# Mem rows turned with six products, ones written as four-byte words, and a new order for units 0 to 2

## The chip, the cores and the metric

The kernel runs on one core of a Trainium2 chip. The metric is the device time of one execution in microseconds (us). The kernel before takes 224.45 us, the median of three runs (224.44 to 224.99). A core has five engines that each work through a queue of their own in order: PE (matrix products; its weight loads run ahead of them), DVE (vector operations), ACT (activations, copies), POOL (vector operations; here it also issues nearly all loads) and SP (here it issues stores and a few copies). They wait for each other by semaphores.

## The reference

Two layers on 4 sequences of 768 tokens, 8 heads of 64 values. First a chunked attention: queries of a chunk of 32 tokens see 8 memory rows, 16 tokens to the left of the chunk, the chunk, and 8 tokens to the right.

```python
k_full = np.concatenate([mem_k, k_ctx], axis=2)
v_full = np.concatenate([mem_v, v_ctx], axis=2)
scores = scale * np.matmul(q_c, k_full.transpose(0, 1, 3, 2))
a = np.exp(scores - np.max(scores, axis=-1, keepdims=True))
a = a / (np.sum(a, axis=-1, keepdims=True) + 1e-09)
out[:, :, c_start:c_end] = np.matmul(a, v_full)
```

Then, with the heads side by side (512 values for each token), a normalised two-layer network with a residual:

```python
xn = (x - mu) / np.sqrt(var + 1e-06) * g_ln
out = x + np.maximum(xn @ w_ch1, 0.0) @ w_ch2      # 512 -> 2048 -> 512
```

## The kernel before

Tokens are worked in 24 blocks `t` of 128 (six for each sequence `b`), and the network in 12 units `u` of 256 tokens, so unit `u` has blocks 2u and 2u+1. One block goes through these steps, each a small function:

- `qk_products(t)` (PE, 32 small matmuls, L322): scores from the turned queries `QD` and the turned keys `KT`; `row_max` and `less_max` (DVE, L331 and L334); `weights` (ACT, exp, L344).
- `pt_products(t)`, `pt_copy`: the weights turned on PE and copied out of PSUM (L353, L361).
- `val_products(t)` (PE, L373): weights by `V`. `V` has a column of ones beside each head's values, so that the same product gives the sum of the weights. `tokens(t)` (DVE, L382 to L389) divides by it and takes the mean.
- `shift(t)` (POOL L396 or ACT L400) subtracts the mean, `x_products` turns the block on PE (L429), `x_copy` (DVE, L445) takes it out of PSUM into `xT`. `square` (ACT) and `root_of` (POOL) make the scale that is applied at the very end.

A unit then has eight `up_products(u, s)` (PE, L464, 8 matmuls of 256 columns each), each followed by a relu on ACT or DVE into `rT` (`relu_up`, L456 and L458), and its down products: unit 0 by eight `down_products` (L490), later units by seven `down7_products` (L643), a scheme with fewer products for which sums of `w2` blocks (`w2_sum`, DVE, L619) and of `rT` blocks (`r_sum`, DVE, L637) are needed. `down_add` and `add_to` (DVE, L498, L650) add the result to the block, and `store` sends it off.

Inputs come as raw rows. `load_octets(i, half, src, ...)` (L107) loads half of K (i = 0), Q (1) or V (2) of one sequence into `raw`, for two parities of heads one after the other; the loads turn float32 into float16. For the first half of the first sequence, K and Q are turned on PE straight from `raw` (`turn`, L228); else `mix_into` (L261, on DVE, ACT or POOL) joins the two parities first, and `turn_whole` turns them (L274). `to_stream` (L241) and `to_rows` (L249) take the result out of PSUM into `KT` and `QD`. V of the first sequence is turned as well, into `VT`, where its rows can be shifted, and turned back by `v_products(g)` and `v_copy(g)` (L296, L307) for 12 groups `g` of 64 tokens. V of later sequences is loaded in place by `load_v_group`. The memory rows of K (32 rows of 8 x 64 values) and of V's first sequence (8 rows) are loaded on SP, cast on ACT (L722), turned by `mem_products` (L193) and spread into `KT` and `VT` by `mem_cols` and `mem_ends`.

Eight PSUM banks hold the results: `one`, `upb` and `dnb` with two each, and `two` (two banks) for the values. A product waits until the former content of its bank has been copied out.

All of it runs in an order written out by hand (`manual_schedule`): the order of the calls is the order in each engine's queue. Units 0 to 2 are one long list of calls, from L721 to the end of the list; it ends with the last down products of unit 1 and the last up products of unit 2. Then a loop with a plan runs units 3 to 7, and another list the rest. `warm(n)` puts n products of zeros on PE.

Of the kernel before, what the change touches and what calls it, by code (L numbers as in the profile page):

```python
# [14 lines left out]
TOP = 3.4028234663852886e38  # L15


@with_exitstack
def kernel(
# [38 lines left out]
    MR = B * H + H  # L58
    mem32 = T[1].bitcast(FP32).rearrange("p n (x c) -> p (n x) c", c=64)[0:MR, 0:8, :]
    mem16 = T[0].rearrange("p n (x c) -> p (n x) c", c=64)[0:MR, 0:8, :]  # L60
# [114 lines left out]
    def load_mem(queue, lo, src, n, off=0, step=512):  # L175
        queue.dma_start(
            out=mem32[lo : lo + n], in_=dram(src, off, [[step, n], [1, 512]])
        )

# [7 lines left out]

    def mem_products(p):

        half = MR // 2  # L190
        for m in range(8):
            for par in range(2):
                nc.tensor.matmul(  # L193
                    out=p[64 * par : 64 * par + 64, half * m : half * m + half],
                    lhsT=mem16[:, m, :],
                    rhs=free(identity[0:MR, :], 2 * par, [[4, half // 2], [1, 2]]),
                    start=True, stop=True, tile_position=(0, 64 * par),
                )

    def mem_copy(p, engine):  # L200
        half = MR // 2
        copy_on(engine)(out=memT, in_=free(p, 0, [[1, half], [half, 8]]))
# [504 lines left out]
    load_mem(nc.sync, 0, mem_k, B * H)  # L707
    load_mem(nc.sync, B * H, mem_v, H)
# [3 lines left out]
    for i in range(2):  # L712
        nc.vector.memset(V[i][:, :, :, 64:VW], 1.0)
# [8 lines left out]
    copy_on("A")(out=mem16, in_=mem32)  # L722
    load_octets(0, 0, k, 0, 0, 48, (0,))
    load_octets(0, 0, k, 0, 0, 48, (1,))
    make_identity(nc, identity)
    mem_products(upb[1])
    warm(6, one[0])
    tk1 = turn(raw[0][0], 1, 48, one[0])
    load_octets(1, 0, q, 0, 0, 32, (1,))
    mem_copy(upb[1], "A")  # L730
    load_octets(1, 0, q, 0, 0, 32, (0,))
    mem_cols(VT, memT[:, 16:20, :], "V")
    tk0 = turn(raw[0][0], 0, 48, upb[0])
    warm(1, one[1])
    tq1 = turn(raw[1][0], 1, 32, one[1])
    to_rows(0, tq1, 1, "A", 32, 0, 16, 32)
    mem_cols(KT[0], memT[:, 0:4, :], "A")
    tq0 = turn(raw[1][0], 0, 32, dnb[1])
    to_rows(0, tq0, 0, "A", 32, 0, 16, 32)
    to_stream(KT[0], tk1, 1, "V", 48, 0)  # L740
    load_octets(2, 0, v, 0, 0, 48, (0,))
    to_stream(KT[0], tk0, 0, "V", 48, 0)
    warm(4, dnb[0])
    s1 = qk_products(1, dnb[0])
    to_rows(0, tq0, 0, "A", 32, 0, 0, 16)
    load_octets(2, 0, v, 0, 0, 48, (1,))
    mix_into(whole[0], raw[2][0], 1, 96, "V")
    mix_into(whole[0], raw[2][0], 0, 96, "A")
    tv1 = turn_whole(whole[0], 1, 96, upb[1])
    load_octets(2, 1, v, 0, 48, 48, (1,))  # L750
    row_max(1, s1)
    to_stream(VT, tv1, 1, "A", 48, 0)
    nc.gpsimd.memset(last, 1.0)
    tv0 = turn_whole(whole[0], 0, 96, one[0])
    to_stream(VT, tv0, 0, "A", 48, 0)
    mem_ends(KT[0], memT[:, 0:4, :], "V")
    to_rows(0, tq1, 1, "V", 32, 0, 0, 16)
    s0 = qk_products(0, upb[0])
    load_octets(2, 1, v, 0, 48, 48, (0,))
    load_octets(1, 1, q, 0, 32, 64, (1,))  # L760
    mix_into(whole[2], raw[2][1], 0, 96, "V")
    tV0 = turn_whole(whole[2], 0, 96, dnb[1])
    v1 = v_products(1, one[1])
    row_max(0, s0)
    less_max(0, s0)
    v_copy(1, v1, "V")
    v3 = v_products(3, upb[1])
    v0 = v_products(0, one[0])
    less_max(1, s1)
    v_copy(0, v0, "V")  # L770
    load_octets(0, 1, k, 0, 48, 48, (0,))
    load_octets(0, 1, k, 0, 48, 48, (1,))
    mix_into(whole[1], raw[0][1], 0, 96, "V")
    to_stream(VT, tV0, 0, "A", 48, 48)
    v_copy(3, v3, "A")
    v2 = v_products(2, upb[0])
    load_octets(1, 1, q, 0, 32, 64, (0,))
    load_w1(0)
    load_w1(2)
    load_w1(1)  # L780
    weights(0)
    load_w1(3)
    p0 = pt_products(0, dnb[1])
    weights(1)
    pt_copy(0, p0, "V")
    v_copy(2, v2, "V")
    p1 = pt_products(1, one[1])
    mix_into(whole[2], raw[2][1], 1, 96, "A")
    load_w2(0)
    val_products(0)  # L790
    tokens(0)
    mix_into(whole[3], raw[1][1], 1, 128, "A")
    tV1 = turn_whole(whole[2], 1, 96, upb[1])
    to_stream(VT, tV1, 1, "A", 48, 48)
    mix_into(whole[3], raw[1][1], 0, 128, "P")
    load_w2(1)
    tQ0 = turn_whole(whole[3], 0, 128, dnb[0])
# [4 lines left out]
    tQ1 = turn_whole(whole[3], 1, 128, one[0])  # L802
    to_rows(0, tQ0, 0, "A", 64, 32)
    pt_copy(1, p1, "V")
    val_products(1)
    load_octets(0, 0, k, 1, 0, 48, (0,))
    copy_on("V")(
        out=V[0][96:128, NG - 1, :, 64:VW],
        in_=free(last[96:128, 0:1], 0, [[0, H], [0, VW - 64]]),
    )  # L810
    to_rows(0, tQ1, 1, "A", 64, 32)
    mix_into(whole[1], raw[0][1], 1, 96, "V")
    tK1 = turn_whole(whole[1], 1, 96, dnb[1])
    tokens(1)
    shift(0, "P")
    x0 = x_products(0, upb[0])
    x_copy(0, x0)
    to_stream(KT[0], tK1, 1, "V", 48, 48)
    shift(1, "A")
    tK0 = turn_whole(whole[1], 0, 96, one[1])  # L820
    to_stream(KT[0], tK0, 0, "A", 48, 48)
    load_octets(0, 0, k, 1, 0, 48, (1,))
    square(0)
    x1 = x_products(1, upb[1])
    load_v_group(1, 9, 1)
    x_copy(1, x1)
    v6 = v_products(6, dnb[0])
    v5 = v_products(5, one[0])
    square(1)
    v_copy(5, v5, "V")  # L830
    root_of(0)
    v4 = v_products(4, upb[0])
    v_copy(4, v4, "V")
    load_w2(2)
    load_w2(3)
    v10 = v_products(10, dnb[1])
    v_copy(10, v10, "V")
    s2 = qk_products(2, one[1])
    row_max(2, s2)
    load_mem_rows(1, B)  # L840
    up_products(0, 0, upb[1])
    relu_up(0, 0, upb[1], "V")
    up_products(0, 5, one[0])
    relu_up(0, 5, one[0], "A")
    load_v_group(1, 8, 1)
    less_max(2, s2)
    weights(2)
    load_v_group(1, 7, 1)
    load_octets(1, 0, q, 1, 0, 48, (0,))
    up_products(0, 2, upb[0])  # L850
    relu_up(0, 2, upb[0], "A")
    up_products(0, 4, dnb[1])
    relu_up(0, 4, dnb[1], "A")
    p2 = pt_products(2, upb[1])
    pt_copy(2, p2, "V")
    up_products(0, 1, one[1])
    relu_up(0, 1, one[1], "A")
    load_octets(0, 1, k, 1, 48, 48, (1,))
    v7 = v_products(7, one[0])
    v_copy(7, v7, "A")  # L860
    s3 = qk_products(3, upb[0])
    row_max(3, s3)
    less_max(3, s3)
    v8 = v_products(8, dnb[1])
    load_octets(0, 1, k, 1, 48, 48, (0,))
    v9 = v_products(9, upb[1])
    v_copy(9, v9, "A")
    val_products(2)
    tokens(2)
    shift(2, "P")  # L870
    mix(0, 0, "P")
    up_products(0, 3, one[1])
    relu_up(0, 3, one[1], "V")
    load_v_group(1, 1, 0)
    v_copy(6, v6, "V")
    w2_sum(0)
    weights(3)
    up_products(0, 7, one[0])
# [583 lines left out]
```

## Time and profile before

| What | Value |
|---|---|
| Median of three runs | 224.45 us |
| The profiled execution | 224.56 us |
| Its span (first to last instruction) | 222.8 us |
| PE busy | 213.6 us (96%) |
| DVE busy | 178.3 us (80%) |
| ACT busy | 132.0 us (59%) |
| POOL busy | 128.2 us (58%) |
| First product of real inputs on PE (K turned) | at 8.09 us |
| First up product of unit 0 | at 24.88 us |
| First up product of unit 3 | at 71.69 us |
| Granted PE clock, mean | 0.992 |

The profile is one execution. Times are from the start of the span. Busy time of an engine is the union of its instructions; that of PE is modelled at its ends and can hide short waits. The granted clock is the share of PE's full clock. DMA share is the mean busy share of 16 DMA engines, and a load's time to landing counts from the start of its issue. The first 40 us are a period of heavy loading: from the second to the ninth of the page's 40 slices the DMA engines are busy for nine tenths or more.

### The profile page before, as it was taken

What the parts mean: (1) busy time and instruction counts of PE and PEld (TensorE: products, weight loads), DVE (VectorE), ACT (ScalarE), POOL (GpSimd) and SP (SyncE); (2) the same over time, 40 slices, a digit from 0 to 9 for tenths busy, and PEclk for the clock granted to TensorE, in tenths of its full rate; (3) what the DMA queues carried; (4) which work ended last, traced back from release to release, by engine and by line L of the source; (5) the groups of instructions that cost most, each with busy time, mean ns of one, the idle gap of its engine ahead of it and who ended that gap; (6) DMA issues with size and microseconds to landing.
All of it is one profiled execution on the core that took longest, in us unless ns stands there. A gap on an engine that the chain in (4) does not pass through costs nothing.

```text
span 222.8 us, 8324 instructions
## 1 busy us (share of the span) xinstructions
PE 213.6 (96%) x3578; PEld 188.3 (84%) x3578; DVE 178.3 (80%) x396; ACT 132.0 (59%) x260; POOL 128.2 (58%) x203
## 2 busy tenths in 40 slices
PE   6977999998999999999999999999999999999993
PEld 2456895698999989999999999999898999999982
DVE  6587956897898987896686996895789987788983
ACT  3297766677786388468447278378757743654100
POOL 7937327888989726976454937415277548930000
PEclk9996999999999999999999999999999999999999
DMA  4999999999984993994952992952100011101115
GB/s 76 183 191 207 213 205 208 189 136 133 137 52 57 206 162 68 130 74 113 157 73 57 144 131 59 107 98 63 50 3 3 3 47 50 47 4 49 47 56 184
DMA packets 43450, 23.24 MB, mean 104 GB/s; under 512 B 30004, under 2 KB 39796, under 8 KB 43364
## 3 DMA queue, kind: packets, MB, share of 16 engines
q0 software_dynamic: 38416, 14.48, 56.8%
q1 hardware_dynamic: 4996, 8.22, 12.7%
q8 instruction: 28, 0.46, 0.8%
q14 instruction: 10, 0.08, 0.1%
HBM read 29.02 MB, written 6.29 MB: 158 GB/s over the span
## 4 chain that ended last, share of the span: by engine, by line
PE 85%; DMA 4%; POOL 4%; DVE 3%; issue 1%; ACT 1%; DVEq 0%; POOLq 0%
PE upb L464 22%; PE dnb L643 20%; PE one L464 6%; PE one L643 5%; DMA raw<-in_q_dram 4%; PE upb L643 4%; PE two L373 4%; PE one L274 3%; POOL raw L107 3%; PE dnb L464 2%; PE dnb L578 2%; PE one L578 2%; PE one L429 2%; PE one L322 2%; PE dnb L490 2%; PE upb L490 2%
## 5 line engine op out<-in xcount | busy, mean ns | idle before, releaser
L464 PEld LDWEIGHTS <-w1c 128*128 128x128 f16 x640 | 67.4, 114 | 1.7
L464 PE MATMUL upb<-xT,w1c 128*128 128x256 f16 x448 | 58.3, 273 | 0.0
L456 ACT ACTIVATE rT<-upb 128x512 f16<-128x512 f32 x53 | 30.9, 595 | 17.6 <-PE upb L464 17.6
L650 DVE SCALAR_TENSOR_TENSOR xs<-dnb,rstd,xs 128x256 f32<-128x256 f32 x54 | 25.9, 479 | 11.3 <-PE dnb L643 9.5
L643 PEld LDWEIGHTS <-RS 128*128 128x128 f16 x320 | 30.4, 98 | 3.2
L344 ACT ACTIVATE P<-sub 128x512 f16<-128x512 f32 x24 | 15.0, 633 | 25.0 <-DVE sub L334 25.0
L416 POOL TENSOR_SCALAR veps<-ssq 128x1 f32<-128x1 f32 x24 | 5.6, 235 | 36.9 <-ACT sq L409 36.1
L643 PEld LDWEIGHTS <-rT 128*128 128x128 f16 x240 | 22.9, 98 | 2.3
L643 PE MATMUL dnb<-T,RS 128*128 128x256 f16 x184 | 23.9, 273 | 0.0
L396 POOL TENSOR_SCALAR xn<-xs,nmean 128x512 f16<-128x512 f32 x18 | 13.8, 768 | 14.8 <-DVE nmean L389 11.5
L637 DVE TENSOR_TENSOR RS<-rT 128x1024 f16<-128x1024 f16 x18 | 13.5, 754 | 5.4 <-ACT rT L456 5.4
L464 PE MATMUL one<-xT,w1c 128*128 128x256 f16 x136 | 17.4, 273 | 0.0
L409 ACT ACTIVATE sq<-xs,nmean 128x512 f16<-128x512 f32 x24 | 17.3, 720 | 0.1
L383 DVE CUSTOM_DVE_ANT_1 xs<-two,rec 128x512 f32<-128x512 f32 x24 | 16.6, 691 | 0.8
L420 POOL TENSOR_TENSOR rstd<-veps,mhalf 128x1 f32<-128x1 f32 x24 | 13.5, 563 | 2.0
L643 PE MATMUL dnb<-w2c,rT 128*128 128x256 f16 x112 | 14.4, 272 | 0.0
L116 POOL DMA_DIRECT2D V<-in_v_dram x16 | 13.6, 848 | 0.7 <-PE dnb L643 0.6
L456 ACT ACTIVATE rT<-one 128x512 f16<-128x512 f32 x15 | 9.1, 606 | 5.8 <-PE one L464 5.7
L445 DVE TENSOR_TENSOR xT<-one,g_col 128x512 f16<-128x512 f16 x14 | 9.6, 686 | 3.6 <-PE one L429 3.4
L249 ACT COPY QD<-one 128x768 f16<-128x768 f16 (+2 forms) x12 | 9.4, 784 | 5.0 <-PE one L228 4.1
L274 PEld LDWEIGHTS <-raw 96*128 96x128 f16 x192 | 10.5, 98 | 1.5 <-issue 1.2
L373 PEld LDWEIGHTS <-PT 64*32 64x32 f16 x768 | 7.4, 94 | 5.0 <-issue 3.3
(192 smaller groups left out, 479.6 us busy)
## 6 DMA issues: line engine op xcount, KB each, us to landing
out_dram<-xs SPq DMA_DIRECT2D x23, 256.0 KB, 2.1
raw<-in_k_dram POOLq DMA_DIRECT2D x16, 192.0 KB, 6.6
raw<-in_q_dram POOLq DMA_DIRECT2D x12, 192.0 KB, 7.1
w1c<-in_moe_w_ch_dram POOLq DMA_DIRECT2D x4, 512.0 KB, 13.4
w2c<-in_moe_w_ch_dram POOLq DMA_DIRECT2D x4, 512.0 KB, 14.5
V<-in_v_dram POOLq DMA_DIRECT2D x16, 77.0 KB, 3.8
raw<-in_v_dram POOLq DMA_DIRECT2D x4, 192.0 KB, 5.7
V<-memv SPq DMA_DIRECT2D x6, 120.0 KB
```

The costliest lines, as they stand in the source:

```text
L116: nc.gpsimd.dma_start(out=V[b % 2][72:128, 0 : NG - 1, h, 0:64], in_=dram(v, base + 16 * D, [[64, 56], [64 * 64, NG - 1], [1, 64]]),)
L274: nc.tensor.matmul(out=pv[:, rows * r : rows * r + rows], lhsT=m[0:rows, jj, r, :], rhs=identity[0:rows, 0:rows], is_transpose=True, start ...
L344: nc.scalar.activation(out=P[t % 3], in_=sub[t % 2], func=ACTF.Exp, scale=0.125)
L373: nc.tensor.matmul(out=two[col : col + 32, 128 * h : 128 * h + 65], lhsT=PT[t % 3][rows, 2 * (h // 4) + h % 2, q0 : q0 + 32], rhs=V[b % 2] ...
L383: nc.vector.tensor_tensor_reduce(out=x.rearrange("p (h d) -> p h d", h=H), in0=free(two, 0, [[128, 8], [1, 64]]), in1=free(r, 0, [[1, 8], ...
L396: nc.gpsimd.tensor_scalar(out=xn[i], in0=x, scalar1=m, scalar2=1.0, op0=ALU.add, op1=ALU.mult,)
L409: nc.scalar.activation(out=sq, in_=xs[t % 9], func=ACTF.Square, bias=nmean[t % 6], scale=1.0, accum_out=ssq[i],)
L420: nc.gpsimd.tensor_tensor(out=rstd[t % 9], in0=veps[i], in1=mhalf, op=ALU.pow)
L456: nc.scalar.activation(out=o, in_=i, func=ACTF.Relu)
L464: nc.tensor.matmul(out=p[:, 256 * hb : 256 * hb + 256], lhsT=free(w1c[hc // 4][:, dt, :], hc % 4, [[4, 128]]), rhs=xT[u % 3][:, dt, :], st ...
L643: nc.tensor.matmul(out=p[:, 0:256], lhsT=left[:, n, :], rhs=right(n), start=(n == 0 and not add), stop=(n == 7), skip_group_check=add,)
L650: nc.vector.scalar_tensor_tensor(out=x, in0=p[:, 0:256], scalar=rstd[t % 9], in1=x, op0=ALU.mult, op1=ALU.add,)
```

## The change

Four edits to what runs, and one to the order.

1. The mem rows are loaded as rows of 64 values (128, 128 and 64 of them), so that six products turn them and no longer sixteen. ACT casts them in two pieces, and DVE, not ACT, takes the result out of PSUM.
2. The ones beside the values in `V` and `memv16` are written as four-byte words: two float16 values that are nearly one, as one float32 number of the same bits. That halves the elements of these fills.
3. These fills no longer stand at the head of DVE's queue. They are calls in the list: `V[0]` on POOL behind two w1 loads, `V[1]` on DVE in the middle of unit 0, `memv16` on DVE behind the load of the mem values.
4. The number of warming products goes from 7 + 6 + 1 + 4 to 7 + 6 + 1 + 6.
5. The list of units 0 to 2 has a new order, with other engines for some of the copies and relus, other PSUM banks, and another order of the loads.

```diff
+ONES = 0.007826805114746094
-    MR = B * H + H
-    mem32 = T[1].bitcast(FP32).rearrange("p n (x c) -> p (n x) c", c=64)[0:MR, 0:8, :]
+    mem32 = T[1].bitcast(FP32).rearrange("p n (x c) -> p (n x) c", c=64)[:, 0:3, :]
...
+    def mem_cast(engine):
+        copy_on(engine)(out=mem16[:, 0:2, :], in_=mem32[:, 0:2, :])
+        copy_on(engine)(out=mem16[0:64, 2, :], in_=mem32[0:64, 2, :])
+
     def mem_products(p):
-        half = MR // 2
-        for m in range(8):
+        for x, rows, n in ((0, 128, 8), (1, 128, 8), (2, 64, 4)):
             for par in range(2):
                 nc.tensor.matmul(
-                    out=p[64 * par : 64 * par + 64, half * m : half * m + half],
-                    lhsT=mem16[:, m, :],
-                    rhs=free(identity[0:MR, :], 2 * par, [[4, half // 2], [1, 2]]),
+                    out=p[64 * par : 64 * par + 64, 64 * x : 64 * x + 8 * n],
+                    lhsT=mem16[0:rows, x, :],
+                    rhs=free(identity[0:rows, :], 16 * par, [[32, n // 2], [1, 16]]),
...
+    def ones_into(i, engine):
+        set_on(engine)(V[i].bitcast(FP32)[:, :, :, 32 : VW // 2], ONES)
+        set_on(engine)(V[i][0:16, 0, :, 64:VW] if i == 0 else V[i][0:16, 0, :, :], 0.0)
+        set_on(engine)(V[i][96:128, NG - 1, :, :], 0.0)
+
+    def ones_into_mem(engine):
+        set_on(engine)(memv16.bitcast(FP32)[:, :, :, 32 : VW // 2], ONES)
...
-    load_mem(nc.sync, 0, mem_k, B * H)
-    load_mem(nc.sync, B * H, mem_v, H)
+    nc.sync.dma_start(
+        out=mem32[:, 0:2, :], in_=dram(mem_k, 0, [[64, 128], [8192, 2], [1, 64]])
+    )
+    nc.sync.dma_start(out=mem32[0:64, 2, :], in_=dram(mem_v, 0, [[64, 64], [1, 64]]))
...
-    for i in range(2):
-        nc.vector.memset(V[i][:, :, :, 64:VW], 1.0)
-        nc.vector.memset(V[i][0:16, 0, :, 64:VW] if i == 0 else V[i][0:16, 0, :, :], 0.0)
-        nc.vector.memset(V[i][96:128, NG - 1, :, :], 0.0)
-    nc.vector.memset(memv16[:, :, :, 64:VW], 1.0)
```

The order of POOL's queue, from its start to w2's last chunk, before and after (`k0` is K's first half of the first sequence, `k1` its second half, and so on; two loads each, one for each parity; a load of w1 or w2 is one chunk of four):

```
before: k0 k0, identity, q0 q0, v0 v0 v1 (last) v1, q1, k1 k1, q1, w1: 0 2 1 3, w2: 0,
        join q1, w2: 1, next k, shift 0, next k, V group, root 0, w2: 2 3
after:  k0 k0, q0, identity, q0, v0 v0 v1, q1, v1 (last), q1, k1 k1, w1: 2 0, ones V[0],
        join v1, w1: 3, join q1, join v1, w1: 1, shift 0, shift 1, w2: 0 1 2 3
```

PE's order from its start to the end of unit 0's up products (`tk`, `tq`, `tv` turns of first halves, `tK`, `tQ`, `tV` of second halves, `s` scores, `p` turned weights, `val` values, `x` turned blocks, `v` V products):

```
before: warm 7, mem, warm 6, tk1 tk0, warm 1, tq1 tq0, warm 4, s1, tv1 tv0, s0, tV0, v1 v3 v0 v2,
        p0 p1, val0, tV1, tQ0 tQ1, val1, tK1, x0, tK0, x1, v6 v5 v4 v10, s2,
        up 0 5 2 4, p2, up 1, v7, s3, v8 v9, val2, up 3 7 6
after:  warm 7, warm 6, tk1 tk0, mem, warm 1, tq0 tq1, warm 6, tv1 tv0, s0 s1, v3 v1 v0 v2 v4,
        p0, tV1, tQ0, val0, tQ1, p1, tV0, val1, tK0, x0, tK1, x1, v6 v5 v11 v10, s2, v7,
        up 5 1 0, p2, up 6, v9, s3, val2, v8, up 4 7 2 3
```

In the new list DVE has the relus of up products 5, 1, 7 and 2 of unit 0 and 6 of unit 1, where it had 0 and 3 of unit 0 and 7 of unit 2; ACT has more of the V and weight copies. The last stretch of the list differs in order only.

More of the change, by code (lines that the diff above doesn't have):

```diff
@@ L734 @@
[L734 to L740, printed above, removed]
+    warm(6, one[1])
+    tk1 = turn(raw[0][0], 1, 48, one[1])
+    tk0 = turn(raw[0][0], 0, 48, upb[0])
+    mem_products(dnb[0])
+    mem_copy(dnb[0], "V")
+    mem_cols(VT, memT[:, 16:20, :], "V")
+    mem_cols(KT[0], memT[:, 0:4, :], "V")
@@ L769 @@
[L769 to L787, printed above, removed]
@@ L817 @@
+    shift(1, "P")
+    x1 = x_products(1, one[1])
     x_copy(0, x0)
+    v6 = v_products(6, upb[0])
     to_stream(KT[0], tK1, 1, "V", 48, 48)
[L819 to L831 removed]
```

566 lines of the change are left out of this document (297 added, 269 removed).

## The prediction

> **What bounds the kernel now.** I read four views in this order: the stages (busy time of each engine in stretches that I chose), the chain that ended last, the order of time of the first 72 us, and the time to landing of each load.
>
> Stages. The columns are length, then busy time of PE, weight loads, DVE, ACT and POOL, then the granted clock, the DMA share and GB/s:
>
> ```profile
> 15.49:18.90 3.41, 1.76 (x50) 1.22 (x51) 2.53 (x10) 2.84 (x6) 1.19 (x2) 1.00 1.24 206
> 18.90:22.31 3.41, 3.41 (x62) 3.12 (x62) 2.11 (x8) 2.56 (x4) 3.01 (x6) 0.50 1.24 206
> 22.40:71.70 49.30, 48.10 (x917) 41.05 (x915) 39.88 (x85) 35.83 (x73) 36.30 (x60) 1.00 1.13 147
> 24.87:71.69 46.82, 46.06 (x853) 39.40 (x841) 37.41 (x81) 33.40 (x68) 36.11 (x59) 1.00 1.12 144
> 71.69:219.28 147.59, 147.36 (x2338) 136.01 (x2336) 122.21 (x270) 83.15 (x164) 76.29 (x113) 1.00 0.52 79
> ```
>
> Three parts are to be seen. From 71.69 us, where the first product of unit 3 starts, to 219.28, where the last matmul ends, PE is busy for 147.36 of 147.59 us. Nothing there is changed, so a microsecond won or lost before 71.69 should arrive at the end whole. Between 24.87 (first up product) and 71.69 PE looks full as well, but its busy time is modelled and hides short waits. Before 24.87 PE is partly idle, and for 3.41 us its clock is halved, behind a stretch in which it was busy for 1.76 of 3.41 us.
>
> The chain that ended last, in order of time (start, length, what):
>
> ```profile
> 8.56 9.10 DMA raw<-in_q_dram
> 17.71 1.05 POOL T L261
> 18.80 0.98 PE dnb L274 x8
> 24.94 0.99 PE upb L464 x8
> ```
>
> The last load of Q lands at 17.66, POOL joins it, PE turns it, and everything queued behind that turn on PE is late: the values of token blocks 0 and 1, their transposes, the first up product.
>
> Order of time: start, length, engine, line, operation, tiles, and the idle time ahead:
>
> ```profile
> 1.46 1.34 DVE L713 MEMSET V<- 128x1536 f16 x1 [0.27 <-issue]
> 3.77 1.34 DVE L713 MEMSET V<- 128x1536 f16 x1 [0.37 <-issue]
> 4.88 0.60 PE L193 MATMUL upb<-identity,T 40*64 40x20 f16 x16 [0.47 <-ACT T L722]
> 5.42 2.74 PE L703 MATMUL one<-zeros 128*128 128x512 f16 x6
> 8.09 0.78 PE L228 MATMUL one<-identity,raw 96*64 96x96 f16 x16
> 11.93 0.74 POOL L165 DMA_DIRECT2D w1c<-in_moe_w_ch_dram  x1 [0.75 <-DMA raw<-in_v_dram]
> 37.02 0.70 POOL L396 TENSOR_SCALAR xn<-xs,nmean 128x512 f16<-128x512 f32 x1
> 46.73 0.76 DVE L261 COPY raw<-raw 96x1024 f16<-96x1024 f16 x2 [0.15 <-DMA raw<-in_q_dram]
> 46.87 1.09 POOL L396 TENSOR_SCALAR xn<-xs,nmean 128x512 f16<-128x512 f32 x1
> ```
>
> Loads. Each issue with its time to landing gives: first halves of K 6.38, Q 8.27, V 10.15; second half of V 12.72; the rest of K and Q 17.66; w1 chunks 20.2, 23.3, 25.9, 28.9; w2 chunks 30.8, 33.3, 37.9, 40.5. They land in the order of issue, about 2.5 us for 512 KB. POOL issues the n-th load only once the (n-8)-th has landed (the wait at 11.93 ends with V's landing at 11.65), so POOL's order sets what arrives when.
>
> **The change, part by part.**
>
> *Mem rows.* Sixteen matmuls took 0.60 us (about 0.037 each), six take about 0.2. They stood between two groups of warming products, and PE waited 0.47 us for the cast. Now 13 warming products run without a break: 1.25 + 13 x 0.43 = 6.8, and K's turn starts there instead of at 8.09; K has landed at 6.38. Those 1.3 us end in another wait: V's first half lands at 10.15 in both kernels, and the list needs it before the first scores. I book 0. If that cover were absent it would be the 1.3 us. The loads of the mem rows become 320 pieces of 256 B instead of 40 of 2 KB; between nothing and a delay of K by 0.4 us (a fifth of the 2.1 us from the old issue at 0.80 to ACT's start at 2.92), and PE's warming hides that (6.4 + 0.4 against 6.8). ACT casts two pieces instead of one, 0.62 us at most, before it has anything else to do. Booked 0.
>
> *Ones beside V.* DVE loses 1.34 x 2 + 0.11 + 0.33 x 3 + 0.48 = 4.3 us before 6.6, where it only waits for K afterwards: worth 0. What comes back later is no longer hidden by the loads. V[0] goes to POOL, ahead of three of its joining copies: 768 words and two smaller pieces. POOL's fill of 128 elements takes 0.22, its copy of 1024 takes 1.04, so I estimate 1.8 us, bounds 1.0 and 3.0. POOL issues w1's second load at about 10.2 and is done by 12.8, while its next copy waits for V's second half (now one load later, about 14.1): hidden, with 1.3 us to spare. V[1] and the mem values stay on DVE in the middle of unit 0: 768 words (half of 1.34, 0.7), 0.33 + 0.33, and 0.3, together 1.6 us of DVE.
>
> *Loads reordered.* The bytes up to the last w2 chunk lose the next batch's two K loads (1.0 us each) and one V group (0.25), so w2 should be complete at 38.3 instead of 40.5. w1's fourth chunk stays at 28.9; POOL issues w1's third after one copy (about 15.9) and the fourth after two more (about 18.9), long before the queue drains at 23.3. w2's four issues come right behind, about 22, where two of them used to wait until 25.48. Six later issues of V groups and of the next batch's K and Q each keep the eight-deep rule; POOL's `shift(2)` stands behind a load that waits for w1's fourth chunk (28.9), earlier than block 2's values (32.0), so it costs nothing. `root_of(0)` and `root_of(1)` stand behind one that waits for w2's first (31.3); only the additions at 42 need them. On SP the copies within V[1] and the mem rows' copies swap places; both are wanted by the values of block 6 at about 60, and not before.
>
> *From 10 us to the first up product.* Walked through with the rows' durations: a join on DVE 0.42 and on POOL 1.04, a stream on ACT 0.86 and on DVE 1.0, row maximum and difference 0.69 each, weights 0.6, a copy of V or of weights on ACT 0.6, block values on DVE 1.13, shift on POOL 0.75, a transpose's copy-out 0.69. V joined on DVE 10.65, turned 12.1 and 12.5 (behind six more warming products); ACT writes both K streams by 12.3 and V's second stream by 13.5; the first V products 13.6; scores' maxima and differences on DVE end 14.8 and 16.6; weights 16.0; first transposed weights 16.3; Q's second half (15.4, no longer last) joined on DVE 17.0 and turned 17.5; values of block 0 18.2, of block 1 20.4; their shift on POOL 22.6; both transposes out of PSUM 24.2. PE's busy share from 15.49 to 18.90 comes to 1.9 of 3.41, like the row above that precedes the halved clock, so I put 0.4 on this: first up product 24.6 against 24.87. Two more V products (7 and 11, 0.24 each) are then done.
>
> *From there to unit 3.* PE's work in the old stretch, start to start: 24 up products of 0.87, 8 down of 0.86, 7 of 0.87, 4 V products of 0.24, 7 scores of 0.34, 6 + 6 transposes of 0.22, 6 values of 0.26, 8 turns of 0.35: 44.3 of 46.8, so 2.5 us are short waits. The new stretch has 43.8. Its waits: walked bank by bank, 1.4 us (before the fourth up product's copy-out, the last w2 chunk, and the last two transposes). To this I add 0.7 for DVE: work moved between DVE and ACT (V copies -0.4, relus +1.4, weight copies -0.8, one pair of joins +0.8, ones +1.6) make +2.6 on the 39.88 busy us of that stretch, from 81% to about 88%. Bounds: 1.0 (neighbouring DVE operations overlap by 0.08: a 0.68 us maximum at 25.54, the next start at 26.14) and 5.0 (every added DVE us is paid). I take 2.1, near the lower end since the walk goes by full durations.
>
> Sum: 24.6 + 43.8 + 2.1 = 70.5 against 71.69, **1.2 us earlier**. The profiled execution took 224.56, 0.11 above the median 224.45 of the runs, and its span 222.8; the forecast is 224.5 - 1.2 = **223.3**.
>
> *A rule that speaks against it.* POOL's shift took 0.70 us alone and 1.09 beside two DVE copies (46.73 to 47.49): they got in each other's way, 0.39. The new list puts three POOL joins (1.04 each) and two shifts beside DVE joins between 14 and 22 us. The Trainium skill, SBUF — State Buffer, section "Who interferes with whom", says why: DVE's fast copies and GpSimd share one port pair and whoever comes second waits for the whole instruction; these two rows agree. By that rule without overlap the sum would be some 71.5.
>
> **The rivals.**
>
> B, no change: the copies collide. Two or three collisions at 0.4 lie on the path (Q's join at 16.6 beside POOL's join of the other part; K's joins at 19.6 beside the first shift): +1.0, unit 3 at 71.5, 224.3. For it the pair of rows above; against it that some of them fall on work with slack. That the edit does little is the same case: its memsets and mem products are off the chain today.
>
> C, slower: DVE becomes the bound in units 0 to 2. Before, it was idle for 9.4 of 49.3 us, mostly waiting for PE. If it goes on waiting half as often as the added 2.6 us need, unit 3 starts at about 73.0: 224.5 + 1.3 = 225.8. It decides from the point where DVE's idle time in that stretch falls below some 6 us. For it: every copy-out that frees a bank for PE now queues behind a relu or a fill on DVE. Against it: ACT lost what DVE got, and the old waits of DVE were for PE.
>
> D, faster than forecast: PE keeps its full clock, since 13 unbroken warming products and the earlier work fill it. The halved stretch cost up to 1.7 us of PE time; half of that is on the path: 222.4.
>
> **How the numbers follow.** A 0.5 (223.3; own range 222.7 to 223.8), B 0.19 (224.3), C 0.23 (225.8), D 0.08 (222.4). 0.3% is 0.67 us, about what a measurement of this kernel tells from no change. Faster: A without its upper end, and D, 0.55. Within: B and that end, 0.21. Slower: most of C, and B's tail, 0.24. The range from 222.2 to 225.8 leaves out the far end of C and a better D.
>
> **What would show it.** First up product at 24.6 and unit 3 at 70.5, with the stretch behind unchanged at 147.6 us: A. DVE or POOL copies over 0.6 and 1.2 us between 15 and 21: B. DVE over 90% busy from 22 to 70 with PE waiting for copies of PSUM banks: C. No halved clock: D. The last w2 chunk at 38.3 is the step on the loads; K's turn at 6.8 that on the mem rows. The forecast is wrong if w1 lands later than 28.9, if POOL's fill passes 3 us, or if the stretch from unit 3 grows.

## The result and the profile after

The changed kernel takes 227.58 us, the median of 11 runs (224.93 to 229.82); beside it the kernel before took 224.44 us (224.09 to 224.99, 11 runs). The ratio is 1.0119, with a 95% interval of 1.0088 to 1.0149: slower by about 3 us, where 1.2 us less was forecast. The new kernel also spreads more: its runs cover 4.9 us, those of before 0.9 here and 3.0 in the 31 runs beside the first experiments. A median counts all runs, while a ratio leaves out those over 1.5% above the fastest of their kernel: two of the eleven here (228.99 and 229.82), five of the ten in the first experiment (227.05 to 228.81) and one of the twelve in the last (227.06).

The profiled execution took 227.58 us (span 225.9, mean granted clock 0.985). Its stages, with the columns of the stage view before (length; busy time of PE, weight loads, DVE, ACT, POOL; granted clock, DMA share, GB/s):

```profile
15.19:18.61 3.42, 1.34 (x32) 1.04 (x27) 3.39 (x5) 3.12 (x6) 3.42 (x4) 1.00 1.24 205
18.61:22.02 3.41, 2.90 (x54) 2.61 (x55) 2.57 (x8) 1.01 (x1) 1.24 (x3) 0.50 1.24 206
22.02:25.43 3.41, 2.05 (x64) 1.71 (x63) 2.64 (x9) 3.08 (x7) 1.89 (x3) 1.00 1.24 206
25.43:28.85 3.42, 3.42 (x78) 2.74 (x76) 1.81 (x4) 1.71 (x3) 3.42 (x7) 0.50 1.10 186
28.64:74.66 46.02, 45.63 (x827) 38.86 (x826) 40.51 (x86) 32.78 (x68) 36.66 (x60) 1.00 1.01 131
74.66:222.26 147.60, 147.39 (x2338) 135.96 (x2336) 121.98 (x269) 83.67 (x165) 75.27 (x111) 1.00 0.52 79
```

The last two rows are as forecast: 147.60 us from unit 3 to the last matmul (147.59 before), and 46.02 from the first up product to unit 3 (46.82 before, 45.9 forecast). The loss is all ahead of them: the first up product starts at 28.64, not at 24.88, and so unit 3 starts at 74.66, not at 71.69. The first four rows show two stretches of 3.41 us at half clock where there was one. DVE is full from 15.19 to 18.61, while PE works for 1.34 us.

The chain that ended last shows the start of the loss, in order of time:

```profile
10.96 1.97 DVE T L270 x2
16.90 2.18 DVE T L270
19.12 1.03 PE dnb L283 x8
28.71 1.94 PE one L473 x16
58.63 6.35 DMA V<-in_v_dram
```

Before, the last load of Q and POOL's join stood here. Now two joins on DVE (L270 is the line of `mix_into`) do, with 1.97 us for two and 2.18 for one, and further down a load of V. The order of time shows why (start, length, engine, line, operation, tiles, idle time ahead):

```profile
10.96 1.96 DVE L270 COPY T<-raw 96x1024 f16<-96x1024 f16 x2 [0.87 <-DMA raw<-in_v_dram]
11.14 0.74 POOL L165 DMA_DIRECT2D w1c<-in_moe_w_ch_dram  x1 [0.21 <-issue]
11.88 0.76 POOL L206 MEMSET V<- 128x768 f32 x1
12.97 0.52 PE L283 MATMUL dnb<-identity,T 96*128 96x96 f16 x8 [1.02 <-DVE T L270]
16.76 2.02 POOL L270 COPY T<-raw 128x1024 f16<-128x1024 f16 x2
16.90 2.17 DVE L270 COPY T<-raw 128x1024 f16<-128x1024 f16 x1
19.12 1.03 PE L283 MATMUL dnb<-identity,T 128*128 128x128 f16 x8 [1.61 <-DVE T L270]
25.15 2.17 POOL L171 DMA_DIRECT2D w2c<-in_moe_w_ch_dram  x4
25.91 0.68 DVE L454 TENSOR_TENSOR xT<-one,g_col 128x512 f16<-128x512 f16 x1
28.64 2.01 PE L473 MATMUL one<-xT,w1c 128*128 128x256 f16 x16
65.03 0.42 PE L382 MATMUL two<-V,PT 64*32 64x65 f16 x30 [0.31 <-DMA V<-in_v_dram]
```

DVE's second join of V (the second of the two at 10.96) takes 1.62 us; it ends at 12.92, 0.28 behind the end of POOL's fill of `V[0]`. DVE's join of Q starts 0.14 behind two joins of POOL and ends 0.29 behind the second of them, after 2.17 us. A join of this size on DVE takes 0.42. DVE's copies were held while POOL's fill and joins ran, and PE waited for what DVE had to write (1.02 and 1.61 us). Later the first up product starts 2.05 us after the last copy-out of its unit (25.91 + 0.68 = 26.59), since the V products and scores ahead of it run at half clock (a V product took 0.64 us here, 0.39 in the first experiment).

### The profile page after: what moved, and what is told of

Same layout as the page of the kernel before. It is cut to its first block, busy times and chain, and to the rows that moved or that the text cites. A ratio compares the mean times of both kernels' runs of the same rounds, so it can differ in the third digit from the quotient of the medians.

```text
span 225.9 us, 8306 instructions
## 1 busy us (share of the span) xinstructions
PE 213.2 (94%) x3570; PEld 188.6 (84%) x3570; DVE 178.8 (79%) x390; ACT 130.8 (58%) x262; POOL 133.2 (59%) x208
## 3 DMA queue, kind: packets, MB, share of 16 engines
q1 hardware_dynamic: 5284, 8.22, 12.5%
## 4 chain that ended last, share of the span: by engine, by line
PE 82%; DMA 5%; POOL 5%; DVE 5%; issue 1%; ACT 0%; DVEq 0%; POOLq 0%
PE dnb L652 20%; PE upb L473 20%; PE one L473 5%; PE upb L652 5%; PE one L652 4%; PE two L382 4%; PE dnb L473 3%; DMA V<-in_v_dram 3%; PE one L283 3%; DMA raw<-in_v_dram 3%; PE dnb L587 2%; PE one L587 2%; PE one L331 2%; DVE T L270 2%; PE one L438 2%; POOL raw L107 2%
## 5 line engine op out<-in xcount | busy, mean ns | idle before, releaser
L473 PE MATMUL upb<-xT,w1c 128*128 128x256 f16 x432 | 56.0, 273 | 0.0
L405 POOL TENSOR_SCALAR xn<-xs,nmean 128x512 f16<-128x512 f32 x19 | 15.0, 790 | 26.0 <-DVE nmean L398 22.2
L425 POOL TENSOR_SCALAR veps<-ssq 128x1 f32<-128x1 f32 x24 | 6.4, 266 | 34.8 <-ACT sq L418 34.0
L418 ACT ACTIVATE sq<-xs,nmean 128x512 f16<-128x512 f32 x24 | 17.3, 722 | 1.0 <-DVE nmean L398 0.9
L652 PE MATMUL dnb<-w2c,rT 128*128 128x256 f16 x120 | 15.4, 273 | 0.0
L429 POOL TENSOR_TENSOR rstd<-veps,mhalf 128x1 f32<-128x1 f32 x24 | 14.1, 588 | 2.0
L473 PE MATMUL one<-xT,w1c 128*128 128x256 f16 x112 | 14.3, 274 | 0.0
L473 PE MATMUL dnb<-xT,w1c 128*128 128x256 f16 x96 | 12.4, 274 | 0.1
L343 DVE TENSOR_TENSOR sub<-one,nmx 128x512 f32<-128x512 f32 x17 | 11.7, 689 | 0.5
L340 DVE TENSOR_REDUCE nmx<-one 128x8 f32<-128x512 f32 x17 | 11.6, 685 | 0.4 <-PE one L331 0.3
L382 PE MATMUL two<-V,PT 64*32 64x65 f16 x768 | 10.8, 193 | 0.6 <-ACT PT L370 0.3
```

The costliest lines, as they stand in the source:

```text
L382: nc.tensor.matmul(out=two[col : col + 32, 128 * h : 128 * h + 65], lhsT=PT[t % 3][rows, 2 * (h // 4) + h % 2, q0 : q0 + 32], rhs=V[b % 2] ...
L405: nc.gpsimd.tensor_scalar(out=xn[i], in0=x, scalar1=m, scalar2=1.0, op0=ALU.add, op1=ALU.mult,)
L418: nc.scalar.activation(out=sq, in_=xs[t % 9], func=ACTF.Square, bias=nmean[t % 6], scale=1.0, accum_out=ssq[i],)
L429: nc.gpsimd.tensor_tensor(out=rstd[t % 9], in0=veps[i], in1=mhalf, op=ALU.pow)
L473: nc.tensor.matmul(out=p[:, 256 * hb : 256 * hb + 256], lhsT=free(w1c[hc // 4][:, dt, :], hc % 4, [[4, 128]]), rhs=xT[u % 3][:, dt, :], st ...
L652: nc.tensor.matmul(out=p[:, 0:256], lhsT=left[:, n, :], rhs=right(n), start=(n == 0 and not add), stop=(n == 7), skip_group_check=add,)
```

## The experiments

The theory from these views: the held joins on DVE make the first up product late, and the waits of PE that they cause let its clock fall for a second stretch. The rivals: the order of the loads and of SP's copies; the new clock stretches as a cause of their own; or an edit that was thought harmless. All ratios are to the kernel before, run beside.

### The fill of V[0] off POOL

It goes to the head of DVE's queue:

```diff
+    ones_into(0, "V")
     nc.vector.memset(VT[:, :, 0:16], 0.0)
...
-    ones_into(0, "P")
```

> The changed kernel with one step moved: the fill of V[0] with ones goes from POOL (behind w1's second load) to the head of DVE's queue, where DVE waits for K. Theory 1 (a POOL operation that writes SBUF holds up DVE's fast copies): the second join of V's first half takes 0.42 us and not 1.62, its turn starts at about 12.0 and not 12.97, DVE reaches the join of Q about 1 us earlier and before POOL's own join of Q, so that it no longer takes 2.17 either; first up product at about 25.7 instead of 28.64, total 225.0. Theory 2 (the halved clock makes the loss; the held copies only delay work that has slack): first up product moves by less than 0.5 us, total 227.2. Theory 3 (the new order itself is slow): the copies may get shorter, and the total stays within 0.7 us of the changed kernel's 227.6.

Measured: 226.78 us (223.57 to 228.81, 10 runs), ratio 1.0013 (0.9965 to 1.0061). By the medians of all runs that is 0.8 us better than the changed kernel, by the ratios 1.06%. The five lower runs (up to 226.50) had a granted clock of 0.996 to 1.000, the five upper ones (from 227.05) one of 0.990 to 0.992, which one halved stretch gives: half of 3.41 us is 0.8% of the span. The profiled execution took 224.88 us, and its order of time shows:

```profile
11.05 0.76 DVE L270 COPY T<-raw 96x1024 f16<-96x1024 f16 x2 [0.92 <-DMA raw<-in_v_dram]
16.02 0.43 DVE L270 COPY T<-raw 128x1024 f16<-128x1024 f16 x1
16.76 2.02 POOL L270 COPY T<-raw 128x1024 f16<-128x1024 f16 x2
22.78 0.68 DVE L454 TENSOR_TENSOR xT<-one,g_col 128x512 f16<-128x512 f16 x1
23.89 1.94 PE L473 MATMUL one<-xT,w1c 128*128 128x256 f16 x16
59.86 0.19 PE L382 MATMUL two<-V,PT 64*32 64x65 f16 x1
61.99 0.42 PE L382 MATMUL two<-V,PT 64*32 64x65 f16 x31 [1.94 <-DMA V<-memv]
```

No join is held: those of V take 0.76 together, and Q's starts at 16.02, ahead of POOL's at 16.76. Without the first collision the second does not happen either, in this execution. The clock stays full, and the first up product starts at 23.89, ahead of the forecast 24.6. That settles the first link: without the fill on POOL the join of V is not held, and in this pair of executions the start is 4.75 us earlier, the clock's part included. But the time did not follow: unit 3 starts at 71.64, since the values of block 6 now wait 1.94 us for the mem rows in `V[1]`, and the runs still spread over 5 us. Was that spread the join of Q, held in some executions only? One more execution of the same kernel:

> The kernel with V[0]'s fill on DVE once more, for another look: its executions went from 223.6 to 228.8. Theory: DVE's join of Q at 16.0 us races with POOL's joins; where it comes second it is held for about 2 us, PE waits, and a halved window follows. So an execution over 226.5 has the join over 1.5 us long, one under 225 has it at 0.43. Rival: the spread has another place, behind unit 3, with the join at 0.43 in either case.

It took 226.51 us, its first up product started at 25.51, and Q's join lasted 0.67 us: begun 0.44 ahead of POOL's, it was not held for POOL's whole run. Instead there are a halved stretch from 17.3 to 20.7, a wait of 1.49 us for a load of `V[1]` at 62.8, and a stop of PE of 1.04 us at 116.7. The spread has several sources; the halved stretch is one, and the held join need not be among them.

### The join of Q off DVE

```diff
-    mix_into(whole[3], raw[1][1], 0, 128, "V")
+    mix_into(whole[3], raw[1][1], 0, 128, "A")
```

> The changed kernel with one step on another engine: the join of Q's first parity pair is done by ACT (about 1.04 us) and no longer by DVE (2.17 us while POOL did two joins). Theory 1: no DVE copy over 0.5 us from 16 to 20 us, Q's turn at 17.9 instead of 19.12, first up product at about 27.4, total 226.4. POOL's two joins stay at 1.05 each. Theory 2: the same start of Q's turn, but the total moves only if the number of halved windows does. Theory 3: total unchanged, 227.6.

Measured: 226.25 us (225.02 to 228.24, 10 runs), ratio 1.0086 (1.0048 to 1.0123). In the profiled execution (225.54) V's join is still held for 1.62 us, the clock stays full, the first up product starts at 24.99 and unit 3 at 70.99, near what was forecast. It then loses 1.74 us behind unit 3, in two stops of PE that are told of at the end. In this execution the start is early although V's join is held, as the clock stays full; and the start alone does not set the time.

### The clock

Thirteen warming products in the three waits of PE, and nothing else:

```diff
+    warm(3, one[1])
     p0 = pt_products(0, one[1])
...
+    warm(6, dnb[0])
     tQ0 = turn_whole(whole[3], 0, 128, dnb[0])
...
+    warm(4, one[1])
     x1 = x_products(1, one[1])
```

> The changed kernel with 13 more warming products where PE waits: 3 ahead of the first turned weights, 6 ahead of Q's first turn, 4 ahead of the second turned block (about 2.8 us of PE at full clock, all of it in waits of at least that length). Theory 2: no halved clock after 5 us, or one window fewer at least; the V products and scores at 25.7 to 28.6 take half as long, first up product at about 27.0, total 226.0 and the runs closer together. Theory 1: the held DVE copies are still there (1.62 and 2.17 us) and set the end; less than 0.5 us is won. Theory 3: no change or slower by the added products.

Measured: 225.39 us (224.83 to 226.14, 10 runs), ratio 1.0022 (0.9995 to 1.0049), with the spread down to 1.3 us. Its stages:

```profile
15.00:18.40 3.40, 3.19 (x55) 2.05 (x50) 3.37 (x5) 3.04 (x6) 3.33 (x4) 1.00 1.24 205
18.40:21.80 3.40, 2.91 (x87) 2.07 (x89) 3.16 (x9) 1.98 (x5) 1.76 (x4) 1.00 1.23 206
21.80:25.20 3.40, 3.33 (x88) 2.37 (x74) 3.27 (x9) 3.07 (x6) 2.59 (x5) 1.00 1.25 206
```

The joins are held as before (1.62 and 2.00 us), but the clock stays full, the first up product starts at 26.12 instead of 28.64, and unit 3 at 73.06. About 2 us of the loss thus come by the halved clock; the held joins are still there with the rest. The runs of the changed kernel agree: the one with a granted clock of 1.000 took 224.93, the ten with 0.970 to 0.992 took 226.32 to 229.82. By the medians this is the largest gain of a single edit here, 2.2 us.

Does the old kernel gain by the same means? Seven warming products in its own three waits:

```diff
+    warm(2, dnb[1])
     p0 = pt_products(0, dnb[1])
...
+    warm(2, dnb[0])
     val_products(0)
...
+    warm(3, dnb[0])
     tQ0 = turn_whole(whole[3], 0, 128, dnb[0])
```

> The kernel before with 7 more warming products in its waits of 15 to 19 us (2 ahead of the first turned weights, 2 ahead of the first values, 3 ahead of Q's turn). If a halved window costs about 1.1 us of the total, as the runs of the changed kernel by granted clock suggest: no halved window at 18.9, first up product at about 24.0, total 223.5. If that window has cover (the loads of w1 and w2 set the pace behind it): total 224.3, no change.

Measured: 224.48 us (223.29 to 226.16, 12 runs), ratio 1.0004 (0.998 to 1.0028): no difference. The clock was kept, though: eleven of the twelve runs had a granted clock of 0.997 or more, and of the 29 of the kernel before beside them only nine. The profiled execution took 223.29, the least of all, but two others with 0.999 and 1.000 took 226.15 and 226.16. So the halved stretch costs the old kernel nothing that these medians show, which is what the expectation said for the case that it has cover; what spreads these runs was not traced.

### The edits without the new order

The mem rows and the four-byte words put into the old list, all fills at the head of DVE's queue as in the kernel before:

```diff
-    load_mem(nc.sync, 0, mem_k, B * H)
-    load_mem(nc.sync, B * H, mem_v, H)
+    nc.sync.dma_start(
+        out=mem32[:, 0:2, :], in_=dram(mem_k, 0, [[64, 128], [8192, 2], [1, 64]])
+    )
+    nc.sync.dma_start(out=mem32[0:64, 2, :], in_=dram(mem_v, 0, [[64, 64], [1, 64]]))
...
-        nc.vector.memset(V[i][:, :, :, 64:VW], 1.0)
...
-    nc.vector.memset(memv16[:, :, :, 64:VW], 1.0)
+    ones_into(0, "V")
+    ones_into(1, "V")
+    ones_into_mem("V")
...
-    copy_on("A")(out=mem16, in_=mem32)
+    mem_cast("A")
```

> The kernel before with the other edits alone: mem rows by six products and cast in two pieces, ones as four-byte words, all fills at the head of DVE's queue, the old order of units 0 to 2. All theories: DVE's fills end at about 4.5 instead of 6.6 us and K's turn starts up to 0.4 us earlier, both behind waits for the loads; total 224.4, within 0.3%. If it is slower by over 0.7 us, the smaller pieces of the mem loads or the mem products are a part of the loss, against all three.

Measured: 225.5 us (225.24 to 226.17, 10 runs), ratio 1.0053 (1.0031 to 1.0076). The start was no later (first up product 24.32, unit 3 at 71.52), yet it is slower, which no theory had. So the two edits were run one by one, the fills first:

```diff
-        nc.vector.memset(V[i][:, :, :, 64:VW], 1.0)
...
-    nc.vector.memset(memv16[:, :, :, 64:VW], 1.0)
+    ones_into(0, "V")
+    ones_into(1, "V")
+    ones_into_mem("V")
```

> The kernel before with one edit alone: ones as four-byte words at the head of DVE's queue (no new mem rows). It splits the 1.1 us that the other edits cost in the old order. If the fills are harmless: 224.3, and the loss of the earlier run belongs to the mem rows (smaller load pieces, later or earlier products). If they are not: 225.4 as before, which would have to come from what DVE does earlier than before.

224.42 us (223.88 to 225.48, 10 runs), ratio 0.9999 (0.9979 to 1.0019). And the mem rows alone (with the new `mem_products` of six):

```diff
-    load_mem(nc.sync, 0, mem_k, B * H)
-    load_mem(nc.sync, B * H, mem_v, H)
+    nc.sync.dma_start(
+        out=mem32[:, 0:2, :], in_=dram(mem_k, 0, [[64, 128], [8192, 2], [1, 64]])
+    )
+    nc.sync.dma_start(out=mem32[0:64, 2, :], in_=dram(mem_v, 0, [[64, 64], [1, 64]]))
...
-    copy_on("A")(out=mem16, in_=mem32)
+    mem_cast("A")
```

> The kernel before with the mem rows' edit alone: loads in 256 B pieces, two casts, six products. Theory (e4_old_order's +0.5% is this edit, since the fills alone gave 1.000): 225.3 to 225.9, ratio 1.003 to 1.007. Rival (each edit alone is harmless, e4's loss was another draw of clock windows or an interplay): ratio 0.998 to 1.002, 224.0 to 224.9.

225.69 us (224.66 to 227.29, 6 runs), ratio 1.0082 (1.005 to 1.0115). The loss in the old order is the mem rows' edit, which had been booked at nothing. Where it lies stays open: the one execution with a profile took the least of the six (224.66), and in it the first up product (24.17) and unit 3 (70.82) come earlier than before, while the stretch behind unit 3 is 1.0 us longer (148.55). The largest wait there is one of 0.44 us for DVE at 182.16; with both edits it is one of 0.54 for a load of V at 76.42, so not the same place. K's turn moved from 8.09 to 7.36, so the whole start stands otherwise to the stretches of the clock. That alone is not the cause: all six runs had a granted clock of 0.992 or less, but so had eight of the 17 of the kernel before beside them, and these took 224.16 to 224.87. The edit was not taken back in the changed kernel, so its part of the loss there is not known.

### All three remedies, and the next wait

All fills at the head of DVE's queue, Q's join on ACT, and the thirteen warming products, in the changed kernel:

```diff
+    ones_into(0, "V")
+    ones_into(1, "V")
+    ones_into_mem("V")
     nc.vector.memset(VT[:, :, 0:16], 0.0)
...
-    ones_into(0, "P")
...
-    mix_into(whole[3], raw[1][1], 0, 128, "V")
+    mix_into(whole[3], raw[1][1], 0, 128, "A")
...
+    warm(3, one[1])
...
+    warm(6, dnb[0])
...
+    warm(4, one[1])
...
-    ones_into(1, "V")
...
-    ones_into_mem("V")
```

> The changed kernel with the three remedies together: all fills of ones at the head of DVE's queue, Q's first join on ACT, 13 more warming products in PE's waits. Theory now (held DVE copies make PE wait, and the waits halve its clock; the order of units 0 to 2 itself is good): no DVE copy over 0.6 us before 20 us, no halved clock, first up product at about 24.0, unit 3 at about 70.3, total 223.2, which would beat both kernels. Rival (the new order gives its lead back in the middle stretch, or later loads hold it): first up at 24 and unit 3 not before 71.5, total 224.4 or more.

Measured: 224.12 us (223.48 to 225.77, 12 runs), ratio 0.9982 (0.996 to 1.0004): 3.5 us better than the changed kernel by the medians, level with the one before. Every join on DVE took 0.42 us, the clock was full, and the first up product started at 24.97. But unit 3 started at 72.98 in the profiled execution (225.77, its slowest run), and the order of time says why:

```profile
61.51 0.19 PE L382 MATMUL two<-V,PT 64*32 64x65 f16 x1 [0.71 <-DMA V<-memv]
63.34 0.42 PE L382 MATMUL two<-V,PT 64*32 64x65 f16 x31 [1.64 <-DMA V<-memv]
```

The values of block 6 wait for the copies of the mem rows into `V[1]`, which the new order puts behind the copies within `V[1]` on SP. When SP issued them, before and in the first experiment:

```profile
40.81 1.59 SPq L158 DMA_DIRECT2D V<-memv  x2
53.27 1.50 SPq L158 DMA_DIRECT2D V<-memv  x2
```

Before, they stood ahead of the copies within `V[1]` and went out 20 us ahead of block 6's values (60.82); now they go out behind such a copy, which starts at 52.33. In the changed kernel PE waited only 0.31 us at this place, for a load of V, since all was late by then. The exchange that takes the wait away moves the mem rows' copies (to 45.07) and one of POOL's loads of `V[1]`:

```diff
     to_rows(1, lq01, 1, "A", 48, 0)
-    load_v_group(1, 8, 1)
+    load_v_group(1, 1, 1)
+    v_mem(1)
...
-    load_v_group(1, 1, 1)
+    load_v_group(1, 8, 1)
...
-    v_shared(1, 0, 4)
...
-    v_mem(1)
+    v_shared(1, 0, 4)
```

With the three remedies:

> The kernel of e5_three with the next wait taken away too: the rows of mem are copied into V[1] ahead of the copies within V[1] on SP, and POOL's load of V[1]'s pages for block 6 changes places with a later one. Theory (what e5 gained before unit 0 was eaten by block 6's values, which waited about 2.4 us for these two transfers): the values of block 6 run at about 61.5 without a wait above 0.3 us, unit 3 begins at about 70.5, and the time is about 222.3 to 222.8, below both kernels. Rival (the next late transfer takes their place, here the copies within V[1] or the load put later): a wait of 0.5 us or more for one of these in units 1 to 2, unit 3 at 72 to 73, and the time stays at 224.1.

Measured: 222.9 us (222.66 to 223.3, 6 runs), ratio 0.9909 (0.988 to 0.9937). This is faster than both kernels. The stages, and the values of block 6 in the order of time:

```profile
25.09:70.39 45.30, 45.21 (x828) 38.74 (x825) 39.03 (x82) 32.73 (x68) 37.43 (x61) 1.00 1.11 147
70.39:217.94 147.55, 147.34 (x2338) 135.96 (x2336) 121.85 (x269) 83.58 (x165) 75.25 (x112) 1.00 0.52 80
```

```profile
60.72 0.44 PE L382 MATMUL two<-V,PT 64*32 64x65 f16 x32
```

No wait stands behind the values any more. The first up product is no earlier than with the three remedies (25.09); the stretch from there to unit 3 fell from 48.01 us to 45.30, by 2.7.

The exchange alone, in the changed kernel:

> The changed kernel with that exchange of transfers alone; fills, joins and clock are left as they are. Theory: in the changed kernel the first up product is so late that block 6's values waited only 0.5 to 0.7 us for V[1], so at most that is won: 226.9 to 227.6. Rival (the order of the transfers is the larger part of the loss, and the late joins are not): 224.5 to 225.5.

Measured: 225.9 us (224.93 to 227.34, 10 runs), ratio 1.0047 (1.0023 to 1.0072). That is 0.7% better than the changed kernel, more than the 0.7 us that the theory allowed and less than the rival's. In the profiled execution the stretch to unit 3 is 45.06 us instead of 46.02, where the wait that went was 0.31 us of PE; the first up product is also earlier, at 27.10, with one halved stretch instead of two, although nothing ahead of it was changed. Eight of these ten runs had a granted clock of 0.992 or more, but only two of the changed kernel's eleven, so a part of the gain is the clock's and not the exchange's. Whether the second stretch stayed away by chance is open.

Last, the fastest of these kernels without its warming products:

```diff
-    warm(3, one[1])
...
-    warm(6, dnb[0])
...
-    warm(4, one[1])
```

> The kernel of e9_four without its thirteen warming products. Theory (held joins, idle PE with its halved clock, and V[1]'s late transfers are three losses beside each other): the joins are not held, block 6's values don't wait, but executions with a halved window in the first 30 us come back, each about 1 us longer: first up product at 25 to 26.5, median 223.0 to 224.2 with a wider spread than e9_four's 222.66 to 223.30. Rival (the halved windows came from the waits that the held joins made, so they are gone with the joins): 222.6 to 223.2, as e9_four.

Measured: 224.2 us (223.18 to 227.06, 12 runs), ratio 0.9994 (0.9974 to 1.0014). The spread is back, from 0.6 us to 3.9. The six runs with a granted clock of 0.997 or more took 223.18 to 223.96, the six with 0.992 or less 224.44 to 227.06. The clock is therefore a loss beside the others and not only what the held joins did to it: even with no join held, PE has too many waits in these 30 us to keep its clock in every execution.

## Why the prediction was wrong, step by step

**"From 10 us to the first up product"** is the step that failed: 24.6 forecast, 28.64 measured. The other terms add 0.12, and 223.3 + 4.16 for the later unit 3 (74.66 against 70.5) gives 227.5 us, against 227.58 measured. Within it:

- The joins. The walk took 0.42 for each on DVE, and the rival B priced "two or three collisions at 0.4", from a pair of POOL rows. The mechanism was right and the price far too low: the copy on DVE was held until the next gap in POOL's work, 1.2 us for one fill and 1.75 for two joins without a gap between them. V's second turn on PE ended at 13.49 (12.5 forecast), Q's at 20.15 (17.5).
- The fill of V[0]. Its length was right (0.76 + 0.36 + 0.63 = 1.75 against an estimate of 1.8), and "hidden, with 1.3 us to spare" was worked out for POOL's own queue alone. What it holds on DVE was not asked. Moving it brought the first up product to 23.89 and 25.51 in the two profiled executions; of the time it is worth 0.8 us by the medians and 1.06% by the ratios.
- The halved clock. 0.4 us was put on one stretch. There were two, and the second lies across the products just ahead of the first up product: 2.05 us from the last copy-out to it, where the first experiment has 0.43 (23.46 to 23.89). Some 1.6 us of the 4.0 are this. With warming products, both stretches gone and the joins still held, the first up product came at 26.12: that puts some 2.5 us of the 4.0 on the clock and leaves 1.5 for the held joins. PE's share ahead of the first of them was forecast as 1.9 of 3.41 us and came as 1.34.

The rule that was weighed against the change, in the section "Who interferes with whom" of the page SBUF — State Buffer of the Trainium skill, says that the one who comes second waits for the whole instruction. It was read as "without overlap" and given 1.0 us (71.5 against 70.5). The traces agree with the whole wait: V's join ended 0.28 us behind the fill, and Q's join waited across two joins of POOL (2.17 us). They do not show which came first in the case of V, whose join is recorded 0.58 us ahead of the fill.

**"both are wanted by the values of block 6 at about 60, and not before"** failed as well, but showed only once the start was early again: the mem rows were not there at 60, and PE waited 1.94 us in one run and about 2.4 us in another. Taking this step back, with one load of V, is worth 0.7% by the ratios (0.9982 to 0.9909) and 1.2 us by the medians.

**"Mem rows", booked 0**, is slower by 0.8% alone in the old list. K's turn moved to 7.15 (6.8 forecast), and the gain did end in the wait for V, as said; the loss was not foreseen and is not explained. What it costs in the new order was not run.

Right were: the stretch behind unit 3 (147.60); the stretch from the first up product to unit 3 (46.02 against 45.9), with DVE at 88% as worked out (40.51 of 46.02), so rival C did not come (the 46.02 is in part luck, as below); w1's last landing at 28.52 (28.9). W2 was issued at 25.15 and not at about 22, as POOL's second shift was late too, and its last chunk landed at 39.02, not 38.3, without harm. The 46.02 owes something to the late start: with the first up product at 23.89 and 24.97, near the forecast, it took 47.75 and 48.01, as block 6's values then waited, and 45.30 once that wait was gone. D came out the other way round: the new list did not fill PE, it emptied it.

None of the three signs named as making the forecast wrong came: w1 was in time, POOL's fill took 1.75 us, and the stretch from unit 3 did not grow. What failed stood outside them.

The forecast of 70.5 for unit 3 was reached once the omitted waits were taken away (70.39), at 223.3 us in the profiled execution and 222.9 in the median; that kernel has four edits more than the one that was forecast. The old list gained nothing from the new fills (0.9999) or from warming products (1.0004), and lost by the mem rows (1.0082), so the gain of 0.9% points to the new order itself; the new order alone was not run. It was lost in places that the walk passed with the durations of undisturbed copies.

## What to carry to other kernels

A fill or copy moved to POOL must be costed by what DVE does beside it, not by the slack in POOL's queue: here a copy of 0.42 us on DVE lasted 1.62 and 2.17, until the next gap in POOL's work. When an order gets earlier, go through every transfer behind it with its landing time, as the next late one takes the gain. Where the start of a kernel leaves PE idle for about half of a 3.4 us stretch, a few products of zeros in its waits can keep the clock. In the changed kernel this also gained 2.2 us and narrowed the spread from 4.9 to 1.3 us; in the one before the clock was kept too, and neither the time nor the spread got better. When a kernel's runs split into two groups, set the granted clock of each run beside its time before the median is read.

## What the runs showed of the hardware

**Held copies on DVE.** POOL's fill only writes, and still held a copy of DVE: V's second join took 1.62 us in all four profiled executions with the fill on POOL, and 0.42 or less in the other executions of the new order. In the changed kernel it began at 11.30 and would have ended at 11.72, ahead of the fill's recorded start at 11.88, and was held all the same; in the first experiment the same load issue on POOL without a fill behind it did not hold it (0.41). Why it began so early is open; the profile calls spans on POOL rough. And Q's join, which came first behind the start of POOL's first join, did not get in between the two, which overlap by 0.07 us in the trace (16.76 to 17.80 and 17.73 to 18.78): it ended 0.29 us after the second. In the two other executions in which DVE's join of Q began after POOL's it took 2.00 and 2.30 us. Into the gap of 0.05 us behind the fill (12.64 to 12.69) V's join did get.

**The clock.** The halved stretches last 3.41 us (in one execution two come in a row, 19.06 to 25.89), and they begin and end at whole multiples of it from the first rise of the clock: at 18.61, 22.02, 25.43 and 28.84 in the changed kernel, whose clock rose at 4.95. In the 14 profiled executions, a stretch at full clock in the first 30 us with PE busy for 0.52 of it or less was followed by a halved one each time (six of six: 0.39, 0.46, 0.46, 0.47, 0.49, 0.52); with 0.61 or more never; in between both were seen (0.55, 0.57 and 0.59 kept it, 0.60 lost it twice). These shares are PE's busy time in the trace, by stretches counted from the first rise of the clock. The Trainium skill, TensorE: Matmul & The Clock Gate, section "Part 1: The HAM clock gate (the "warmup" mystery)", gives the same 3.4 us and the factor of two, but names an idle window as what throttles; here one in which PE was idle for about half was enough.

**Stops of PE without a named wait.** In six of the 14 profiled executions PE stopped behind unit 3 at one or both of the same two places of its program, for 0.3 to 1.3 us longer than in the execution of before. The longest in the kernel without warming products (order of time):

```profile
85.23 0.82 PE L473 MATMUL upb<-xT,w1c 128*128 128x256 f16 x6 [0.83 <-issue]
114.18 0.29 PE L331 MATMUL one<-KT,QD 64*32 64x64 f16 x14 [0.38 <-issue]
```

Both break a group of products in the middle and wait for nothing that the trace names. Loads of 16 KB of instructions run near them. At the second place PE was late by 0.1 us or more in eight of the 14 executions, and in these it went on 1.24 to 1.50 us after the end of such a load (here 1.41, after one that ended at 112.77); in the six others that load had ended 1.66 us or more before PE came there. That fits a wait for instructions; no run moved these loads, so it is argued and not shown. The stops make 1.3 us of this execution and 1.7 of the one with Q's join on ACT, and with the clock they are a part of why two executions of one kernel here differ by microseconds.
